# Rows of v with the head as the inner index: a P times V that reads every eighth value

## The chip, the cores and the metric

The kernel runs on one core of a Trainium2 chip. The metric is device time in microseconds (us) of one launch; lower is better. A profile of one execution on the chip stands beside the times.

## The reference

Attention with a local window and block summaries, and behind it a mixture of eight experts with two of them for each token. Only the attention matters here:

```python
B, H, S, D = q.shape                    # 4, 8, 768, 64
block, window = (32, 16)
k_sum = k.reshape(B, H, nb, block, D).max(axis=3)
v_sum = v.reshape(B, H, nb, block, D).mean(axis=3)
scores_l = scale * q @ k^T              # kept where |i - j| < window, else -1e9
scores_s = scale * q @ k_sum^T + log(block)
a = softmax(concat([scores_l, scores_s]))
out = a @ concat([v, v_sum])            # then the experts, on rows of (batch, token)
```

## The kernel before

The 4 x 768 tokens are worked through in 24 tiles of 128 tokens, each of two blocks of 64. A block sees a window of W = 94 keys and the NB = 24 block summaries, so NK = 118 keys. For one block and one head, P times V is a matmul with 118 keys on the partitions, the 64 tokens of P as the stationary operand and 65 columns of v as the moving one: the 64 values of the head and a column of ones, whose product is the sum of the softmax. With 8 heads and 2 blocks that is 16 matmuls for a tile, each of which the chip runs as two records because the type is fp32: 32 in the trace. They stand in `av` at line 329 (`L329`).

v comes from memory as rows of 8 heads x 65 values, 2080 bytes, with the ones already in them. They are used in two ways. `load_vn` (L138) brings a whole batch, six rows to a partition, for `v_sums` (L241), which sums blocks of 32 rows on PE. Its result, copied out of PSUM by DVE or ACT (L249, L247), gives the 24 rows of summaries at the top of six tiles `VW` a batch; further copies spread it over the six, on ACT and POOL for the first batch (L251, L253) and by transfers on chip (`v_rest`, L258) for the others. `v_window` (L263) brings 96 rows of v for one block under those 24 rows. The tiles are called `vw` in the trace, and those that lie in a buffer of the later stage `htl` (that of `load_vn` is `hth`).

The order of work is written out by hand. A loop over the tiles issues, in its turn `t`, the loads of v for tile `t + 2`, the scores of `t + 2`, the transposes of P for `t + 1`, the transposes of x for `t - 1` and P times V for `t`, with gate work of the experts in between at set places. All plain transfers are issued by SP in that order, and each waits for the one eight before it. Other lines that are named below: scores L296, mask L286, transposes of P L316 and their copy to SBUF L319 on ACT, transposes of x L366, gate logits L384, maximum of the scores L303 and normalisation L338 to L344 on DVE, the store of x L361.

Of the kernel before, what the change touches and what calls it, by code (L numbers as in the profile page):

```python
# [8 lines left out]
F32 = mybir.dt.float32  # L9
# [8 lines left out]
B, H, S, D = 4, 8, 768, 64  # L18
BLK, WIN = 32, 16
NB = S // BLK  # L20
P = 128
TS = S // P
NT = B * TS
N = B * S
DM = H * D
# [5 lines left out]
NK = W + NB  # L31
PAD = WIN - 1
KW = S + 2 * PAD + 2
VR = 96
VP = S + VR - 64
# [25 lines left out]
def attn_moe(ctx, tc, qt, kt, vt, wgn, noise, w1, w2, out):  # L61
    nc = tc.nc
# [15 lines left out]
    keep = attn.enter_context(tc.tile_pool(name="keep", bufs=1))  # L78
# [20 lines left out]
    KB, VW, KX = [], [], []  # L99
# [30 lines left out]
        kx_sum(t)  # L130

    flat = [x.rearrange("p f n -> p (f n)").bitcast(F32) for x in HT]
    VN = [flat[0][:, H * (D + 1) * j:H * (D + 1) * (j + 1)] for j in range(TS)]

    def load_vn(b, i):
        rows = vt[b, PAD:PAD + S].rearrange("(p j) h d -> p (j h d)", j=TS)
        c = slice(3 * H * (D + 1) * i, 3 * H * (D + 1) * (i + 1))
        nc.sync.dma_start(flat[0][:, c], rows[:, c])  # L138

    load_q(0)  # L140
# [60 lines left out]
        nc.gpsimd.memset(x[:, :, 0:PAD], 0.0)  # L201
        nc.gpsimd.memset(x[:, :, PAD + S:], 0.0)
    for i in range(2):
        VW += [keep.tile([P, H, D + 1], F32, name=f"vw{4 * i + j}") for j in range(4)]
        VW += [flat[1][:, H * (D + 1) * j:H * (D + 1) * (j + 1)].rearrange("p (h d) -> p h d", h=H)
               for j in range(2 * i, 2 * i + 2)]
    late = []
    XG = []
    for i in range(4):
        x = moe.tile([P, 2 * DM], F16, name=f"xg{i}")  # L210
# [21 lines left out]
            nc.tensor.matmul(o[:, i % 2, 0:P], identb, identb, start=True, stop=True, skip_group_check=True)  # L232
        VO.append(o)

    C4 = 2 * (D + 1)

    def v_sums(b):
        pt = psum.tile([P, HP, P], F32, name="pt", bufs=2).rearrange("p a b -> p (a b)")
        for j in range(TS):
            for g in range(4):  # L240
                nc.tensor.matmul(pt[32 * g:32 * g + NB, 0:C4], ind[:, j, :], VN[j][:, C4 * g:C4 * g + C4],  # L241
                                 start=(j == 0), stop=(j == TS - 1), skip_group_check=True)
        x = [y[0:NB].rearrange("p h d -> p (h d)") for y in VW[(b % 2) * 6:(b % 2) * 6 + 6]]
        for g in range(4):
            i, o = pt[32 * g:32 * g + NB, 0:C4], slice(C4 * g, C4 * g + C4)
            if b:
                nc.scalar.activation(x[0][:, o], i, AF.Copy)  # L247
            else:
                nc.vector.tensor_copy(x[0][:, o], i)  # L249
        if b == 0:  # L250
            nc.scalar.activation(x[1], x[0], AF.Copy)  # L251
            for i in range(2, 6):
                nc.gpsimd.tensor_copy(x[i], x[i % 2])  # L253

    def v_rest(b):
        x = [y[0:NB] for y in VW[(b % 2) * 6:(b % 2) * 6 + 6]]
        for y in x[1:]:
            nc.sync.dma_start(y, x[0])  # L258

    def v_window(blk):  # L260
        b, j = divmod(blk, 2 * TS)
        x = VW[(b % 2) * 6 + j % 6]
        nc.sync.dma_start(x[NB:NB + VR], vt[b, 64 * j:64 * j + VR])  # L263
        return x

    VX = {}

    def v_load(t):
        VX[t] = [v_window(2 * t), v_window(2 * t + 1)]

    SC, PE_, PT, PO, X, XR, XT = {}, {}, {}, {}, {}, {}, {}
# [52 lines left out]
    def av(t):  # L324
        o = PO[t]
        for h in range(H):
            for blk in range(2):
                c = (D + 1) * (h % 4)
                nc.tensor.matmul(o[64 * blk:64 * blk + 64, h // 4, c:c + D + 1],  # L329
                                 PT[t][:NK, h % 2, h // 2, 64 * blk:64 * blk + 64], VX[t][blk][:NK, h, :],  # L330
                                 start=True, stop=True, skip_group_check=True)

    xd_w = []
# [678 lines left out]
    for i in range(2):  # L1012
        load_vn(0, i)
# [9 lines left out]
    kx_sum(0)  # L1023
    q_piece(1)
    at(-0.9, v_sums, 0)

    w_alloc(0)
# [11 lines left out]
    for b in range(B - 1):  # L1039
        for j in range(TS):  # L1040
            at((6 * b + KP[j] if b else KP0[j]) + 0.1, k_piece, b + 1, j)
            if j % 3 == 0:
                at(6 * b + KL[j] if b else -1 + j // 3, load_k, b + 1, j, 3)
        for i in range(2):
            at(VL[b][i], load_vn, b + 1, i)
        at(VS[b] + 0.6, v_sums, b + 1)
        at(VS[b] + 1.02, v_rest, b + 1)
# [46 lines left out]
    for t in range(-2, NT - 1):  # L1094
# [45 lines left out]
        if t >= 0:  # L1140
            av(t)
# [5 lines left out]

    av_space(NT - 1)
    av(NT - 1)
    norm(NT - 2)  # L1150
    norm(NT - 1)
# [7 lines left out]
    for i in range(3):  # L1159
        x = late[0].tile([P, DM], F32, name=f"prev{i}")  # L1160
# [132 lines left out]
    for e in range(1, E):  # L1293
# [10 lines left out]
        d = 7 if e == 1 else 0  # L1304
# [117 lines left out]
def layout(q, k, v, moe_w_gate, moe_w_noise, moe_noise, moe_w1, moe_w2):  # L1422
    import numpy as np

    c = np.ascontiguousarray

    def heads(x):
        return c(x.reshape(B, HP, 2, S, D).transpose(0, 2, 4, 1, 3).reshape(B, 2 * D, HP, S))

    v1 = np.concatenate([v, np.ones((B, H, S, 1), v.dtype)], axis=3)  # L1430
    vp = np.zeros((B, VP, H, D + 1), v.dtype)
    vp[:, PAD:PAD + S] = v1.transpose(0, 2, 1, 3)
    wgn = np.zeros((P, DC, 4 * E), moe_w_gate.dtype)
    wgn[:, :, :2 * E] = np.concatenate([moe_w_gate, moe_w_noise], axis=1).reshape(DC, P, 2 * E).transpose(1, 0, 2)
    return {
        "qt": c(heads(q).reshape(B, 2 * D, HP, TS, P).transpose(0, 3, 1, 2, 4).reshape(B, TS, 2 * D, HP * P)),
        "kt": heads(k), "vt": vp,
        "wgn": c(wgn),
        "noise": c(moe_noise.reshape(NT, P, E).transpose(1, 0, 2)), "w1": c(moe_w1), "w2": c(moe_w2),
    }  # L1440
# [16 lines left out]
```

## Time and profile before

| | |
|---|---|
| median of 3 runs | 676.38 us (675.77 to 677.49) |
| the profiled execution | 674.24 us |
| its span, first to last instruction | 672.4 us |
| mean granted TensorE clock | 0.989 |
| PE, DVE, ACT, POOL busy | 640.2, 491.4, 318.9, 322.7 us |

The attention stage ends near 140 us, when the last P times V has run; what follows is the experts' work. The span does not hold the start and the end of the launch, which is the difference to the profiled execution's time. Busy time is the union of an engine's instructions. An idle time is put down to what ended it.

### The profile page before, as it was taken

To read this page: it belongs to the slowest core of one execution; us is meant where nothing else is said; L and a number is where in the kernel's file an instruction comes from. 1 tells how busy PE (TensorE), PEld (TensorE's weight loads), DVE (VectorE), ACT (ScalarE), POOL (GpSimd) and SP (SyncE) were. 2 spreads that over 40 slices of the span, in tenths; PEclk is the share of its full clock that TensorE was granted. 3 is DMA by queue.
4 is the path that set the end of the run, shared out by engine and by line. 5 is a ranking of instruction groups with operands and counts; after the bars stand their busy time and mean duration, and the time that the engine had idled before them with its cause. 6 is when DMAs were issued, how large, how long until landed. Compare 5 with 4: busy or idle time off the path is not lost.

```text
span 672.4 us, 14084 instructions
## 1 busy us (share of the span) xinstructions
PE 640.2 (95%) x5408; PEld 370.4 (55%) x5408; DVE 491.4 (73%) x905; ACT 318.9 (47%) x679; POOL 322.7 (48%) x459
## 2 busy tenths in 40 slices
PE   7989888979999999999999999999999999999993
PEld 6767667755454654555455446544554555455442
DVE  5648898989789588687958795788678687946410
ACT  2878888844152464156326523542463156326100
POOL 3354334430746646563856376545647551640141
PEclk9999999989999999999999999999999999999997
DMA  8999999869998866627554574567266622431121
GB/s 290 308 282 311 290 314 282 258 141 325 285 213 174 262 166 163 235 97 200 157 174 169 158 205 152 179 158 236 96 175 162 221 83 91 171 110 32 34 80 36
DMA packets 99242, 125.66 MB, mean 187 GB/s; under 512 B 57929, under 2 KB 62801, under 8 KB 99164
## 3 DMA queue, kind: packets, MB, share of 16 engines
q1 hardware_dynamic: 87020, 88.37, 45.0%
q0 software_dynamic: 12144, 36.28, 17.4%
q8 instruction: 45, 0.74, 0.5%
q14 instruction: 33, 0.27, 0.1%
HBM read 87.57 MB, written 26.21 MB: 169 GB/s over the span
## 4 chain that ended last, share of the span: by engine, by line
PE 80%; DVE 7%; DMA 6%; ACT 5%; issue 1%; SPq 0%; POOL 0%; POOLq 0%; DVEq 0%
PE pt L946 36%; PE h L827 26%; PE a L827 4%; PE h L791 4%; PE pt L943 3%; ACT p L310 2%; DMA stg<-in_w_dram 1%; PE pt L316 1%; DMA xg<-xd,tb 1%; DMA vw<-in_vt_dram 1%; DVE rh L541 1%; PE s L296 1%; DVE nm L303 1%; PE pt L241 1%; ACT pts L319 1%
## 5 line engine op out<-in xcount | busy, mean ns | idle before, releaser
L92 POOL DMA_INDIRECT out_dram<-y,tb x48 | 64.9, 1352 | 156.0 <-DVE y L969 147.9
L946 PEld LDWEIGHTS <-hth 128*128 128x128 f16 x768 | 75.0, 98 | 89.1
L92 POOL DMA_INDIRECT xg<-xd,tb x53 | 70.2, 1325 | 45.4 <-DVE oc L567 26.7
L946 PE MATMUL pt<-w2l,hth 128*128 128x512 f16 x376 | 88.8, 379 | 0.0
L946 PE MATMUL pt<-w2h,hth 128*128 128x512 f16 x376 | 88.8, 379 | 0.0
L946 PE MATMUL pt<-w2h,htl 128*128 128x512 f16 x376 | 88.8, 379 | 0.0
L827 PE MATMUL h<-tx,sh 128*128 128x408 f16 x336 | 78.7, 336 | 0.0
L969 DVE SCALAR_TENSOR_TENSOR y<-pt,tb,prev 128x512 f32<-128x512 f32 x42 | 31.5, 749 | 52.0 <-PE pt L946 52.0
L649 DVE SCALAR_TENSOR_TENSOR w2l<-stg,w2h 128x1024 f16<-128x1024 f32 x32 | 48.6, 1528 | 27.9 <-ACT w2h L632 27.9
L946 PEld LDWEIGHTS <-htl 128*128 128x128 f16 x384 | 37.6, 98 | 45.3
L827 PEld LDWEIGHTS <-w1h 128*128 128x128 f16 x448 | 43.2, 98 | 33.8 <-issue 1.4
L696 POOL TENSOR_TENSOR t<-xte 128x816 f32<-128x816 f16 x24 | 41.2, 1741 | 36.8 <-DVE t L652 32.3
L92 POOL DMA_INDIRECT prev<-out_dram,tb x42 | 51.9, 1236 | 12.7 <-issue 12.7
L827 PE MATMUL h<-xte,w1h 128*128 128x408 f16 x224 | 57.0, 336 | 0.0
L358 POOL TENSOR_TENSOR xr<-x,xr 128x512 f16<-128x512 f32 x22 | 25.6, 1163 | 61.0 <-ACT xr L351 27.0
L310 ACT ACTIVATE p<-s,nm 128x118 f32<-128x118 f32 x192 | 53.4, 377 | 0.8
L849 ACT ACTIVATE p<-h 128x408 f32<-128x408 f32 x28 | 14.3, 510 | 73.9 <-PE h L827 72.4
L724 ACT ACTIVATE tx<-t 128x816 f16<-128x816 f32 x28 | 24.0, 879 | 50.8 <-DVE t L652 50.8
L827 PEld LDWEIGHTS <-sh 128*128 128x128 f16 x336 | 32.9, 98 | 25.2 <-issue 0.2
L827 PE MATMUL h<-tx,sl 128*128 128x408 f16 x168 | 42.7, 336 | 0.0
L835 DVE SCALAR_TENSOR_TENSOR htl<-h,hth 128x408 f16<-128x408 f32 x56 | 32.1, 573 | 8.4 <-ACT hth L832 8.4
L677 ACT ACTIVATE sh<-ws 128x1536 f16<-128x1536 f32 x14 | 20.8, 1483 | 35.8 <-DVE ws L652 31.7
(213 smaller groups left out, 1239.9 us busy)
## 6 DMA issues: line engine op xcount, KB each, us to landing
stg<-in_w_dram SPq DMA_DIRECT2D x62, 512.0 KB
hth<-in_vt_dram SPq DMA_DIRECT2D x8, 780.0 KB
vw<-in_vt_dram SPq DMA_DIRECT2D x32, 195.0 KB
q<-in_qt_dram SPq DMA_DIRECT2D x24, 256.0 KB
xd<-xr SPq DMA_DIRECT2D x24, 256.0 KB
out_dram<-prev SPq DMA_DIRECT2D x8, 768.0 KB
kb<-in_kt_dram SPq DMA_DIRECT2D x6, 768.0 KB
htl<-in_vt_dram SPq DMA_DIRECT2D x16, 195.0 KB
```

Of the source, the lines that this page charges most:

```text
L92: return nc.gpsimd.indirect_dma_start(**kw)
L310: nc.scalar.activation(PE_[t][:, a, hp, :], SC[t][:, a, hp, :], AF.Exp, bias=NM[t][:, 1, a, hp:hp + 1], scale=0.125)
L358: engine.tensor_tensor(XR[t][:, DM:], X[t], XR[t][:, 0:DM], op=OP.subtract)
L649: nc.vector.scalar_tensor_tensor(lo, SG[e, i], sc, hi, op0=OP.mult, op1=OP.subtract)
L677: nc.scalar.activation(h, x, AF.Copy, scale=W1S)
L696: nc.gpsimd.tensor_tensor(tt(e, 0 if low else j), xb(e, *i, low), xb(e, *o, low), op=OP.subtract)
L724: nc.scalar.activation(TX[e][:, 0, j - 1], t_of(e, j), AF.Copy)
L791: nc.tensor.matmul(ph[:, :n], w[wn][:, c, f * P:(f + 1) * P], x[:, xo + c, c0:c1], start=(k == 0), stop=(k == 11), skip_group_check=hook i ...
L827: nc.tensor.matmul(o, lhs[a][:, c], rhs[b][:, c], start=start and n == 0, stop=stop and n == 5, skip_group_check=True)
L835: nc.vector.scalar_tensor_tensor(HT[1][:, f, c0:c1], c, 0.0, HT[0][:, f, c0:c1], op0=OP.max, op1=OP.subtract)
L946: nc.tensor.matmul(py, hx[:, f, c * P:c * P + P], w[:, f, :], start=first, stop=final, skip_group_check=True)
L969: nc.vector.scalar_tensor_tensor(y, py[:, :d], gw, pv[:, :d], op0=OP.mult, op1=OP.add)
```

## The change

Rows of v in memory now have the head as the inner index: 64 values of the head dimension, each for 8 heads, 2048 bytes a row. The column of ones is no longer loaded. It stands in the tiles `VW` as the last 8 values of each partition, written once at the start by POOL: 1 in all rows and then 32 in the 24 rows of summaries. P times V of one head takes its 65 columns as every eighth value of the row. Loads and copies of v move 512 values instead of 520, and `v_sums` works on 128 columns instead of 130.

```diff
-    VN = [flat[0][:, H * (D + 1) * j:H * (D + 1) * (j + 1)] for j in range(TS)]
+    VN = [flat[0][:, DM * j:DM * (j + 1)] for j in range(TS)]
     def load_vn(b, i):
-        rows = vt[b, PAD:PAD + S].rearrange("(p j) h d -> p (j h d)", j=TS)
-        c = slice(3 * H * (D + 1) * i, 3 * H * (D + 1) * (i + 1))
+        rows = vt[b, PAD:PAD + S].rearrange("(p j) d -> p (j d)", j=TS)
+        c = slice(3 * DM * i, 3 * DM * (i + 1))
...
-        VW += [keep.tile([P, H, D + 1], F32, name=f"vw{4 * i + j}") for j in range(4)]
-        VW += [flat[1][:, H * (D + 1) * j:H * (D + 1) * (j + 1)].rearrange("p (h d) -> p h d", h=H)
+        VW += [keep.tile([P, D + 1, H], F32, name=f"vw{4 * i + j}") for j in range(4)]
+        VW += [flat[1][:, H * (D + 1) * j:H * (D + 1) * (j + 1)].rearrange("p (d h) -> p d h", h=H)
                for j in range(2 * i, 2 * i + 2)]
+    for x in VW:
+        nc.gpsimd.memset(x[:, D, :], 1.0)
+        nc.gpsimd.memset(x[0:NB, D, :], float(BLK))
...
-    C4 = 2 * (D + 1)
+    C4 = DM // 4
...
-        x = [y[0:NB].rearrange("p h d -> p (h d)") for y in VW[(b % 2) * 6:(b % 2) * 6 + 6]]
+        x = [y[0:NB].rearrange("p d h -> p (d h)")[:, 0:DM] for y in VW[(b % 2) * 6:(b % 2) * 6 + 6]]
...
-        nc.sync.dma_start(x[NB:NB + VR], vt[b, 64 * j:64 * j + VR])
+        nc.sync.dma_start(x[NB:NB + VR].rearrange("p d h -> p (d h)")[:, 0:DM], vt[b, 64 * j:64 * j + VR])
...
-                                 PT[t][:NK, h % 2, h // 2, 64 * blk:64 * blk + 64], VX[t][blk][:NK, h, :],
+                                 PT[t][:NK, h % 2, h // 2, 64 * blk:64 * blk + 64], VX[t][blk][:NK, :, h],
...
-    vp = np.zeros((B, VP, H, D + 1), v.dtype)
-    vp[:, PAD:PAD + S] = v1.transpose(0, 2, 1, 3)
+    vp = np.zeros((B, VP, D * H), v.dtype)
+    vp[:, PAD:PAD + S] = v.transpose(0, 2, 3, 1).reshape(B, S, D * H)
```

The order of the instructions on POOL at the start of the program, before the change, from the last memset of the k buffers on (`xg` is a buffer of the later gather, `kx` the keys of a tile):

```order
L202 MEMSET kb_93 128x4x17
L212 MEMSET xg_163 128x1024
L579 IOTA steps 128x21
L119 COPY kx_96<-kb_92 128x4x94 [waits DMAHW2_49,DMAHW1_49]
L119 COPY kx_96<-kb_92 128x4x94
L253 COPY vw_154<-vw_152 24x520 [waits DVE_49]
```

The same place after the change, the last three of the twelve pairs of memsets and what follows (the first pair stands right behind the memset of `kb_93`):

```order
L208 MEMSET vw_159 128x8
L209 MEMSET vw_159 24x8 [waits Pool_49]
L208 MEMSET htl 128x8
L209 MEMSET htl 24x8 [waits Pool_49]
L208 MEMSET htl 128x8
L209 MEMSET htl 24x8 [waits Pool_49]
L215 MEMSET xg_187 128x1024
L582 IOTA steps 128x21
L119 COPY kx_96<-kb_92 128x4x94 [waits DMAHW2_49,DMAHW1_49]
```

Twenty-four instructions came in between; the copy for the third tile's keys still waits for the loads of k alone.

On PE, in the first P times V and behind it, before the change (the two `vw` are the tile's two blocks):

```order
L329 MATMUL o<-vw_152,pts 64x65 [waits DMAHW0_49]
L329 MATMUL o<-vw_153,pts 64x65 [waits DMAHW1_49]
L329 MATMUL o<-vw_152,pts 64x65
L329 MATMUL o<-vw_153,pts 64x65
L329 MATMUL o<-vw_152,pts 64x65
```

And after it:

```order
L332 MATMUL o<-vw_152,pts 64x65 [waits DMAHW0_49]
L332 MATMUL o<-vw_153,pts 64x65 [waits DMAHW1_49]
L332 MATMUL o<-vw_152,pts 64x65
L332 MATMUL o<-vw_153,pts 64x65
L332 MATMUL o<-vw_152,pts 64x65
```

Nothing moved here: the same matmuls wait for the same transfers, and the row does not show the step between the values. On SP the transfers keep their places too; the window loads are 96x512 instead of 96x520.

## Rows read from the trace of the kernel before

**Rows 1.** The page's first lines: span, and busy time, share of the span and number of instructions of each engine.
```profile
span 672.4 us, 14084 instructions
PE 640.2 (95%) x5408; PEld 370.4 (55%) x5408; DVE 491.4 (73%) x905; ACT 318.9 (47%) x679; POOL 322.7 (48%) x459
```

**Rows 2.** Busy time of each engine in the attention stage and behind it: the stretch, its length, then busy us (and instructions) of PE, PE's weight loads, DVE, ACT and POOL, the granted clock, the DMA share and GB/s.
```profile
20.00:140.00 120.00, 107.88 (x2148) 84.26 (x2142) 98.16 (x282) 103.58 (x323) 57.43 (x89) 1.00 0.93 286
140.00:672.40 532.40, 516.64 (x3030) 272.62 (x3024) 382.61 (x591) 209.51 (x339) 259.88 (x346) 0.99 0.55 161
```

**Rows 3.** PE's instructions in order of time for one turn of the loop over tiles: start, time from the first to the end of the last, line, operation, tiles, shape and count, and in brackets the idle time before it and what ended it.
```profile
62.33 1.15 PE L329 MATMUL o<-htl,pts 118*64 118x65 f32 x32
63.42 1.04 PE L296 MATMUL s<-kx,q 64*64 64x118 f32 x32
64.39 1.27 PE L316 MATMUL pt<-ident,p 128*118 128x128 f32 x8
65.59 0.35 PE L286 MATMUL s<-mask,identb 64*64 64x376 bf16 x4
66.34 1.08 PE L384 MATMUL pt<-xt,wg 128*32 128x128 f32 x32 [0.40 <-ACT pts L319]
67.35 0.66 PE L366 MATMUL pt<-ident,x 128*128 128x128 f32 x4
```

**Rows 4.** Who waited for whom from 20 to 140 us: the waiting engine, tile and line, what ended the wait, us in total, times, the longest.
```profile
POOL xr L358 <- ACT xr L351: 27.0, 10, 4.2
...
DVE r L338 <- PE o L329: 9.0, 6, 3.6
...
PE pt L366 <- ACT pts L319: 3.6, 9, 0.9
...
POOL xr L358 <- DMA vw<-vw: 3.3, 1, 3.3
POOL xr L358 <- DMA xd<-xr: 2.8, 1, 2.8
...
PE pt L384 <- ACT pts L319: 2.3, 4, 0.9
...
PE pt L384 <- issue: 1.1, 1, 1.1
PE pt L241 <- ACT pts L319: 1.0, 2, 0.8
...
PE pt L241 <- issue: 0.9, 1, 0.9
...
DVE xr L355 <- DMA xd<-xr: 0.6, 1, 0.6
```

**Rows 5.** The records of P times V: durations in ns (least, median, most), and the first and last start in us.
```profile
L329 PE MATMUL o<-vw,pts x480: 219/222/271, 22.4 to 136.0; 118*64 118x65 f32 x160
L329 PE MATMUL s<-htl,pts x32: 219/222/223, 139.6 to 140.5; 118*64 118x65 f32 x32
```

**Rows 6.** The same of the gate's matmuls.
```profile
L384 PE MATMUL pt<-xt,wg x192: 272/273/298, 45.8 to 144.3; 128*32 128x128 f32 x192
```

**Rows 7.** The transfers of v in the whole program: target and source, queue, count, KB each.
```profile
hth<-in_vt_dram SPq DMA_DIRECT2D x8, 780.0 KB
vw<-in_vt_dram SPq DMA_DIRECT2D x32, 195.0 KB
htl<-in_vt_dram SPq DMA_DIRECT2D x16, 195.0 KB
```

**Rows 8.** All transfers from 12 to 133 us.
```profile
DMA packets 17729, 35.47 MB, mean 293 GB/s; under 512 B 1939, under 2 KB 5267, under 8 KB 17704
```

**Rows 9.** Transfers from 14 to 17 us, when window loads of v make up nearly all of it.
```profile
DMA packets 434, 0.78 MB, mean 261 GB/s; under 512 B 61, under 2 KB 61, under 8 KB 434
```

**Rows 10.** Transfers from 115 to 117 us, when rows of 2048 bytes of q and of the experts' weights make up nearly all of it.
```profile
DMA packets 412, 0.78 MB, mean 389 GB/s; under 512 B 32, under 2 KB 32, under 8 KB 412
```

**Rows 11.** POOL's instructions at the start of the program, columns as in rows 3.
```profile
2.24 0.29 POOL L184 TENSOR_SCALAR base<-base 128x8 f32<-128x8 f32 x1
2.60 0.21 POOL L186 COPY bs<-base 128x8 f32<-128x8 f32 x1
...
4.34 0.15 POOL L202 MEMSET kb<- 128x68 f32 x1
4.43 0.94 POOL L212 MEMSET xg<- 128x1024 f16 x1
5.33 0.15 POOL L579 IOTA steps<- 128x21 f32 x1
7.76 0.94 POOL L119 COPY kx<-kb 128x376 f32<-128x376 f32 x2 [2.28 <-DMA kb<-in_kt_dram]
20.24 1.28 POOL L253 COPY vw<-vw 24x520 f32<-24x520 f32 x2 [11.54 <-DVE vw L249]
```

**Rows 12.** PE's sums of v for one batch, columns as in rows 3.
```profile
71.54 1.53 PE L241 MATMUL pt<-hth 128*24 128x130 f32 x48 [0.18 <-ACT pts L319]
```

**Rows 13.** The chain of work that ended last, followed back from the end, in order of time around 52 to 75 us: start, length, engine or transfer and line.
```profile
52.54 8.98 DMA stg<-in_w_dram
...
61.59 7.27 DMA vw<-in_vt_dram
...
68.92 5.97 DMA xd<-xr
```

More of the change, by code (lines that the diff above doesn't have):

```diff
@@ L255, in v_rest @@
     def v_rest(b):
-        x = [y[0:NB] for y in VW[(b % 2) * 6:(b % 2) * 6 + 6]]
+        x = [y[0:NB].rearrange("p d h -> p (d h)")[:, 0:DM] for y in VW[(b % 2) * 6:(b % 2) * 6 + 6]]
         for y in x[1:]:
@@ L1428, in heads @@
         return c(x.reshape(B, HP, 2, S, D).transpose(0, 2, 4, 1, 3).reshape(B, 2 * D, HP, S))
-    v1 = np.concatenate([v, np.ones((B, H, S, 1), v.dtype)], axis=3)
-    vp = np.zeros((B, VP, H, D + 1), v.dtype)
-    vp[:, PAD:PAD + S] = v1.transpose(0, 2, 1, 3)
+    vp = np.zeros((B, VP, D * H), v.dtype)
+    vp[:, PAD:PAD + S] = v.transpose(0, 2, 3, 1).reshape(B, S, D * H)
     wgn = np.zeros((P, DC, 4 * E), moe_w_gate.dtype)
```

## The prediction

> **What bounds the kernel now.** I read the page's first lines, then the two halves of the span, then one tile's turn on PE, then who waits for whom. The span is 672.4 us, with PE busy for 95% of it [rows 1]. The change touches only what works with v, so the stretch that counts is the attention stage. [...] Three engines and the transfers are nearly level there; PE is the fullest and has 12.1 us free. From 140 us on nothing reads v.
>
> One turn of PE [rows 3] shows the order: P times V (L329, 1.15 us), the next scores (L296), transposes of P (L316), mask (L286), sometimes gate work (L384), transposes of x (L366), and the next P times V. It runs back to back; the gap is a wait for the copy of the transposed P on ACT. Those waits are 3.6 + 2.3 + 1.0 = 6.9 us between 20 and 140 us, and two more gaps of 1.1 and 0.9 us are put down to issue [rows 4]. Whatever makes L329 longer makes the turn longer, except where it eats such a wait. Engines hardly wait for transfers: DVE waits 0.6 us for a store, and POOL 3.3 and 2.8 us, on a step that waits 27.0 us for ACT alone [rows 4].
>
> **The read of every eighth value.** The matmuls of a tile are the same, 32 records in the same order, and only the moving operand changes: 65 values that lay side by side now lie 32 bytes apart. The 32 take 1.15 us [rows 3]; one alone takes 0.222 us [rows 5], which is the tail of the last, so 1.15 - 0.22 = 0.93 us is the time in which values stream in. That is 32 x 65 / 0.93 = 2.2 values per ns.
>
> No PE instruction of before reads with such a step, so the price is bounded. Below: the step costs nothing, 0. A gain is excluded, since the number of columns is the same. Above: the memory must pass over all bytes between the values. The most that a row shows PE reading is L384, 32 matmuls of 128 columns in 1.08 us, of which 0.27 us is the tail [rows 3, 6]: 32 x 128 x 4 bytes / 0.81 us = 20 bytes per ns and partition. P times V would have to pass over 2.2 x 32 = 72 bytes per ns at its old pace, so it would be 3.6 times slower: 0.93 becomes 3.3 us, +2.4 us a tile. Between ends of 1 and 3.6 I take the geometric middle, 1.9, rounded to 2: +0.93 us a tile, since L384 shows that contiguous reads have about twice the room (5.1 values per ns against 2.2) and that no row shows room for 72. Over 24 tiles: 24 x 0.93 = 22 us more of PE.
>
> [...]
>
> What of the 22 us reaches the end: ACT is not the fullest engine, and a longer P times V gives it time to finish the copies for which PE now waits. I let 6 of the 6.9 us of such waits [rows 4] go, so the stage grows by 22 - 6 = 16 us. Behind the longer L329 stand the scores of the next tile (L296), on which DVE's maximum and then ACT's exponentials wait; DVE's normalisation waits for L329 itself already, 9.0 us in 6 waits [rows 4]. Those are parts of the same turn and add nothing of their own.
>
> **The shorter rows.** 48 window loads of 96 rows and 8 loads of 128 runs [rows 7] lose 32 bytes a row (96 a run): 4608 x 32 + 1024 x 96 = 246 KB out of 35.47 MB in 12 to 133 us [rows 8], 0.7%, or 0.8 us of the queue at its 293 GB/s. That is the least. At most, v's rows reach the pace of rows of 2048 bytes: with nearly only v rows in flight the engines move 261 GB/s [rows 9], with nearly only 2048-byte rows 389 GB/s [rows 10]. 48 x 195 KB is 9.58 MB, 37 us at the one and 24 us at the other rate (9.44 MB), so 13 us less. Either way it frees DMA engines, and what waits for them is the little named above. Cover: v for a tile is asked for two tiles ahead. I count 0 in the likeliest case, where PE is slower still and transfers have more time.
>
> **The small edits.** POOL gets 24 memsets after L202. Small memsets there start 0.09 us apart [rows 11], which gives 24 x 0.09 = 2.2 us as the least; every second one waits on the one before, and a dependent pair of steps on POOL is 0.36 us apart in the same rows (L184 to L186), which gives 12 x (0.09 + 0.36) = 5.4 us as the most. The next POOL work begins at 7.76 us, when k lands, and then POOL idles 11.54 us [rows 11]. At the most the copy at 7.76 starts near 10.9 us, for a third tile whose scores are not due before 20 us. Cost 0; without that idle time it would be up to 3.1 us. The window loads wait on no memset. The sums (L241) have 128 columns instead of 130: 1.5% of 1.53 us in each of four batches [rows 12], under 0.1 us together. The copies on DVE, ACT and POOL shrink from 520 to 512 values: nothing.
>
> **Sum.** The profiled execution took 674.2 us for its span of 672.4; the median of the runs is 676.4, 2.1 us above it. 674.2 + 16 = 690 on the profiled one, 676.4 + 16 = 692.4 as a median. I call 692.
>
> **Rivals.**
> - *Nothing moves*: PE reads every eighth value at the old pace and the lighter queue was hidden anyway. For it: the rate of an fp32 stream here is already low, and L384 shows room for twice the contiguous values. Against: each value now stands 32 bytes from the next. 676 us, within 0.5 us.
> - *Faster*: the old pace holds, and the lighter queue takes away what it holds up: DVE's wait of 0.6 us [rows 4] and PE's issue gaps of 1.1 + 0.9 us [rows 4], if those are late instructions that come over the same DMA engines. The chain of work runs through three transfers from 52.5 to 74.9 us [rows 13], which speaks for it; that hardly an engine idles there speaks against. 676.4 - 2.6 = 673.8 us. It decides if P times V stays under 1.2 us a tile. [...]
> - *A small penalty*: factor 1.3, +0.28 x 24 = 6.7 us, most of it in waits that vanish: 678 to 680 us.
> - *The upper bound*: +2.4 us a tile, 57 us, less 7 us of waits: about 726 us.
> - *The change does not do what it says for transfers*: the v loads have 96 partitions where the fast ones have 128, so their lower rate may come from that and not from 2080 bytes. Then the DMA gain is 0.8 us; this removes the faster case and moves no other.
>
> **How the numbers follow.** Likeliest, factor near 2: 0.48, with its own range 686 to 701 (all 12 us of free time absorbed: 676.4 + 22 - 12 = 686; none absorbed and a factor a little over 2: 676.4 + 24 = 701). Small penalty 0.09. Nothing moves 0.22. Faster 0.15. Upper bound 0.06. The range 674 to 701 leaves out the upper bound, most of the faster case and the edges of the others, about 2 in 10. About 2 us, 0.3%, is what a measurement of this kernel can tell from no change. Faster 0.15, same 0.22, slower 0.48 + 0.09 + 0.06 = 0.63.
>
> **What would show it.** In the trace after, the 32 matmuls of P times V take about 2.1 us a tile instead of 1.15, with one alone near 0.28 us; 1.15 again proves that step wrong and leaves the first two rivals. PE's busy time from 20 us to the end of the stage grows by about 22 us, its waits on ACT's copies shrink, and the last P times V ends 16 us later than its 140.5 + 0.2 us of before [rows 5]. The DMA share of the stage falls. What comes after is shifted and not changed. The forecast fails if the penalty is absent or if the free time of PE takes more of it than 12 us.

## The result, and the profile after

The median went from 676.93 us (675.77 to 678.29) to 683.69 us (683.10 to 684.24): ratio 1.0099, 95% interval 1.0076 to 1.0122. The change costs 6.8 us. The forecast was slower by 15.6 us, so the sign is right and the size is not. The profiled execution of after took 683.36 us. Its line numbers are 3 higher than those of before from L241 on: P times V is L332, the scores L299, the transposes of P L319 and their copy L322, the transposes of x L369, the gate L387.

The page's first lines of after, which answer to [rows 1]:

```profile
span 681.6 us, 14108 instructions
PE 656.5 (96%) x5408; PEld 387.4 (57%) x5408; DVE 490.0 (72%) x905; ACT 320.3 (47%) x679; POOL 323.2 (47%) x483
```

PE's busy time grew by 16.3 us, DVE's and ACT's by nothing. The two stretches of after, columns as in [rows 2]:

```profile
20.00:140.00 120.00, 117.66 (x2015) 95.47 (x2019) 90.29 (x262) 98.44 (x304) 52.21 (x83) 1.00 0.90 277
140.00:681.60 541.60, 523.68 (x3145) 279.18 (x3135) 387.89 (x610) 215.11 (x357) 263.26 (x350) 0.99 0.55 160
```

PE is idle for 2.3 of 120 us, where it was idle for 12.1. The two stretches are equally long, so that of after holds less of the work (2015 records of PE against 2148). The DMA share fell from 0.93 to 0.90, as the same work is spread over more time. A turn of PE in after, columns as in [rows 3]:

```profile
59.40 2.12 PE L332 MATMUL o<-vw,pts 118*64 118x65 f32 x32
61.45 1.04 PE L299 MATMUL s<-kx,q 64*64 64x118 f32 x32
62.41 1.09 PE L319 MATMUL pt<-ident,p 128*118 128x128 f32 x8
...
64.42 2.12 PE L332 MATMUL o<-htl,pts 118*64 118x65 f32 x32
```

P times V takes 2.12 us instead of 1.15, and the scores take what they took; the transposes of P take 1.09 us, where they took 1.27. No gap is left in this turn, which has no gate work. The records of P times V, which answer to [rows 5]:

```profile
L332 PE MATMUL o<-vw,pts x480: 298/299/313, 21.3 to 144.9; 118*64 118x65 f32 x160
...
L332 PE MATMUL s<-htl,pts x32: 298/299/303, 149.1 to 150.9; 118*64 118x65 f32 x32
```

The last P times V ends at 150.9 + 0.3 = 151.2 us instead of 140.7: the stage ends 10.5 us later. Who waited for whom from 20 to 145 us in after, columns as in [rows 4]:

```profile
DVE r L341 <- PE o L332: 18.8, 12, 3.7
ACT pts L322 <- PE pt L319: 11.9, 14, 2.2
...
PE pt L387 <- ACT pts L322: 0.7, 2, 0.5
...
PE pt L369 <- ACT pts L322: 0.5, 3, 0.2
```

The waits have turned round. PE waited 3.6 + 2.3 us for ACT's copies before [rows 4] and waits 0.5 + 0.7 us now; DVE's normalisation waits 18.8 us for P times V where it waited 9.0, and ACT's copies, which waited 2.4 us for PE before, now wait 11.9.

One difference between the profiled executions is not the change's. The profiled execution of before lies 2.7 us below the median of before in this comparison (674.24 and 676.93), that of after 0.3 us below its own. So the traces differ by 9.1 us and the medians by 6.8. Where a size is judged below, the medians decide.

### The profile page after: what moved, and what is told of

It reads as the page before. It is cut to its first block, busy times and chain, and to the rows that moved or that the text cites. A ratio compares the mean times of both kernels' runs of the same rounds, so it can differ in the third digit from the quotient of the medians.

```text
span 681.6 us, 14108 instructions
## 1 busy us (share of the span) xinstructions
PE 656.5 (96%) x5408; PEld 387.4 (57%) x5408; DVE 490.0 (72%) x905; ACT 320.3 (47%) x679; POOL 323.2 (47%) x483
## 4 chain that ended last, share of the span: by engine, by line
PE 89%; DVE 5%; ACT 2%; DMA 1%; issue 1%; SPq 0%; POOL 0%; POOLq 0%; DVEq 0%
PE pt L949 36%; PE h L830 26%; PE o L332 5%; PE a L830 4%; PE h L794 3%; PE pt L946 3%; PE pt L319 3%; PE s L299 3%; PE pt L369 2%; DMA kb<-in_kt_dram 1%; PE pt L244 1%; PE h L949 1%; PE pt L387 1%; ACT p L313 1%; DVE nm L306 1%; ACT pts L322 1%
```

## The experiments

Times are medians, ratios are against runs of before on the same chip, which took 675.89 us beside e1 to e3, 675.02 beside e4 to e7, 677.84 beside e8 to e11 and 677.65 beside e12 and e13. The letters of the theories belong to each expectation; the text names the theories in words.

### e1: the long rows kept, the strided read too

After, with the ones loaded again: rows of 2080 bytes, the head as the inner index, no memsets.

```diff
-    vp = np.zeros((B, VP, D * H), v.dtype)
-    vp[:, PAD:PAD + S] = v.transpose(0, 2, 3, 1).reshape(B, S, D * H)
+    vp = np.zeros((B, VP, (D + 1) * H), v.dtype)
+    vp[:, PAD:PAD + S] = v1.transpose(0, 2, 3, 1).reshape(B, S, (D + 1) * H)
```

> The changed kernel with one part undone: P times V still reads every eighth value, but the rows of v in memory are 2080 bytes again, with the ones in their last 8 values, and the memsets are gone. Theory 1 (the strided read costs 23 us of PE, free time of PE swallows 13 of them, and the length of the rows is worth nothing): 683 to 685 us, as the changed kernel. Rival (the free time swallows only the 6 us that were forecast, and the shorter rows give about 8 us back): 690 to 693 us.

Measured: 681.58 us, ratio 1.0095 (1.0062 to 1.0129), where after has 1.0099. The loss comes with the read; beside it the shorter rows and the memsets show no effect, though the two ratios are compared to no better than about 3 us.

### e2, e10 and e11: the short rows alone

e2 has the rows of 2048 bytes and the ones written on chip, but the heads lie one behind the other and P times V reads 65 values side by side. The 65th column is then another head's value for all heads but the last, so all heads are divided by the sum of head 7. e10 is before with that same division and nothing else; e11 is e2 again, beside e10.

```diff
-  PT[t][:NK, h % 2, h // 2, 64 * blk:64 * blk + 64], VX[t][blk][:NK, h, :],
+  PT[t][:NK, h % 2, h // 2, 64 * blk:64 * blk + 64], VX[t][blk].rearrange("p d h -> p (d h)")[:NK, D * h:D * h + D + 1],
...
-        nc.vector.tensor_scalar(r, o[:, :, :, D], 1e-9, 1.0 / XS, op0=OP.add, op1=OP.mult)
+        nc.vector.tensor_scalar(r, o[:, 1:2, 3:4, D].to_broadcast([P, 2, 4]), 1e-9, 1.0 / XS, op0=OP.add, op1=OP.mult)
```

> The other part alone: rows of 2048 bytes, ones on chip, but with the 64 values of a head side by side, so that P times V reads 65 neighbours as before. The column of ones stands behind the last head only, so all heads are divided by the sum of head 7; the amount of work is the same. Theory 1 (row length is worth nothing where PE sets the pace): 676 to 678 us, like the kernel before. Rival (shorter rows give 6 to 8 us back): 668 to 671 us.

> The kernel before, with all heads divided by the sum of head 7, as in e2, so the output is not that of the reference; nothing else. If e2's 0.3% came from its 2048-byte rows, this takes the time of before within 0.5 us. If it came from the other read of the sums, this is 1.5 to 2.5 us faster than before, as e2 was.

> The same kernel as e2 on the chip of e10 (heads divided by the sum of head 7): 2048-byte rows, ones on chip, contiguous read. If the rows are worth something, 0.2 to 0.4% faster than before and than e10 again; if not, equal to e10.

Measured: e2 673.19 us, ratio 0.9967 (0.9945 to 0.9990). e10 677.00, ratio 0.9991 (0.9961 to 1.0021). e11 674.70, ratio 0.9960 (0.9930 to 0.9990). From e10 to e11 the means of 12 runs each differ by 2.3 us, with an interval of 0.4 to 4.2. So the gain of about 0.3% belongs to the rows with what goes with them (the ones written on chip, 512 values instead of 520), and not to the division. Part of the 2.3 us may be the granted clock: its mean over the runs is 0.9891 in e10 and 0.9902 in e11, and within one kernel the runs with a lower mean are mostly the longer ones (correlation -0.61 in e10 and -0.74 in e11). A straight line through the runs of this chip (about 0.6 us for 0.001, an estimate) leaves 1.6 us, 0.2 to 3.1, for the rows. Beside the strided read no such gain shows, but e1 is not exact enough to exclude it there. Where in the trace it arises is not settled: from 20 to 140 us PE is busy 105.5 us in e10 and 105.4 in e11, and ACT 102.9 and 102.3. From 140 to 160 us the granted clock is 0.91 in e10 and 1.00 in e11, but it is 1.00 in e4 too, which has the long rows.

### e0: what a step costs on PE

Matmuls on constants and nothing else of the kernel. Each group reads its moving operand with a step of 1, 2, 3, 4, 8 or 16 elements, in the shape of P times V (65 fp32 columns on the two 64-column halves of the array in turn), on one half alone, on four quarters, and with fp16 on the whole array.

```python
mf[s] = pool.tile([P, 128, s], F32, name="f" + words[s])
...
nc.tensor.matmul(o[64 * b:64 * b + 64, 0, 0:65], wf[:118, 0:64], mf[s][:118, 0:65, i % s], start=True,
                 stop=True, skip_group_check=True)
```

> Nothing of the program is left but matmuls on constant tiles, to price the read by itself: fp32 in two column strips as in P times V, in one strip and in four, and fp16 over the full array, each with steps of 1, 2, 3, 4, 8 and 16 values. [...] If it hangs on the bytes passed over: steps 2, 3 and 4 already cost, and 16 costs more than 8. If it is a limit of the memory shared by the strips: one strip with step 8 is free, and four strips cost twice what two do.

PE's instructions in order of time, columns as in [rows 3]; the name of the moving tile says the step. First fp32 on both halves, then on one half, then fp16 on the whole array:

```profile
10.30 2.09 PE L86 MATMUL o<-fone,wf 118*64 118x65 f32 x64
12.21 2.09 PE L86 MATMUL o<-ftwo,wf 118*64 118x65 f32 x64
14.13 3.04 PE L86 MATMUL o<-fthree,wf 118*64 118x65 f32 x64
17.00 4.01 PE L86 MATMUL o<-ffour,wf 118*64 118x65 f32 x64
20.83 4.02 PE L86 MATMUL o<-feight,wf 118*64 118x65 f32 x64
24.67 4.13 PE L86 MATMUL o<-fsixteen,wf 118*64 118x65 f32 x64
28.61 2.05 PE L90 MATMUL o<-fone,wf 118*64 118x65 f32 x32
30.49 2.04 PE L90 MATMUL o<-ftwo,wf 118*64 118x65 f32 x32
...
38.93 4.02 PE L90 MATMUL o<-feight,wf 118*64 118x65 f32 x32
42.77 3.79 PE L90 MATMUL o<-fsixteen,wf 118*64 118x65 f32 x32
...
63.98 3.67 PE L99 MATMUL o<-hone,wh 128*128 128x256 f16 x32
67.48 3.79 PE L99 MATMUL o<-htwo,wh 128*128 128x256 f16 x32
71.11 5.59 PE L99 MATMUL o<-hthree,wh 128*128 128x256 f16 x32
76.54 7.42 PE L99 MATMUL o<-hfour,wh 128*128 128x256 f16 x32
83.78 14.63 PE L99 MATMUL o<-height,wh 128*128 128x256 f16 x32
98.23 14.90 PE L99 MATMUL o<-hsixteen,wh 128*128 128x256 f16 x32
```

A group of 32 matmuls on both halves has 64 records in fp32, one of 32 in fp16 has 32. Read the differences of the starts. In fp32 step 2 costs what step 1 costs (1.92 and 1.91 us), step 3 half as much again (2.87), step 4 twice (3.83), and steps 8 and 16 hardly more than step 4 (3.84 us; 4.13 from first to end against 4.01). So from step 4 on the price does not grow with the bytes passed over, which was the prediction's way to its upper bound. At step 8 one half alone needs as long for its 32 records (3.84 us) as both halves for their 64, and at step 1 nearly so (1.88 us against 1.91). One half takes 32 x 65 values in a group: 0.92 ns a value at step 1, 1.84 ns from step 4 on. In fp16 a group is 32 x 256 values: 0.43 ns each at step 1, then 0.44, 0.66, 0.88 and 1.76 ns at steps 2, 3, 4 and 8. Past the steps that cost nothing, the time of a value grows with the step: in fp32 it is 1.38 and 1.84 ns at 12 and 16 bytes, 0.115 ns a byte, and in fp16 0.66, 0.88 and 1.76 ns at 6, 8 and 16 bytes, 0.11 ns a byte (both an estimate from these rows). Beyond 16 bytes it hardly grows in either (in fp16 14.90 us from first to end at step 16 against 14.63 at step 8). Of the expectation, neither a price by the bytes passed over nor a limit shared by the strips came out: step 2 costs nothing and step 16 hardly more than step 8, and one half at step 8 is not free (3.84 us against 1.88 at step 1).

### e4 and e5: the dose of the strided read

e4 interleaves the heads in pairs, so that P times V reads every second value. e5 interleaves heads 0 to 3 by four and leaves 4 to 7 as before, which is half of after's extra work on PE. Both have rows of 2080 bytes with the ones.

```diff
+    lo = v1[:, :4].transpose(0, 2, 3, 1).reshape(B, S, 4 * (D + 1))
+    hi = v1[:, 4:].transpose(0, 2, 1, 3).reshape(B, S, 4 * (D + 1))
+    vp[:, PAD:PAD + S] = np.concatenate([lo, hi], axis=2)
```

> As the run with strided reads and rows of 2080 bytes, but the heads are interleaved in pairs, so that P times V reads every second value (8 bytes apart). By the table of steps this read is free: one tile's P times V takes 1.15 us and the time is that of the kernel before, 675 to 678 us. If any step costs: 679 us or more.

> Rows of 2080 bytes; heads 0 to 3 are interleaved by four (16 bytes apart, the full price by the table of steps), heads 4 to 7 lie side by side. PE has 24 x 0.48 = 11.5 us more to do than before. Theory A (PE's free time of about 13 us in the stage is used up first, and only what is left over arrives): 676 to 678 us. Theory B (a fixed share of about a third arrives, whatever the size): 679 to 681 us.

Measured: e4 674.43 us, ratio 0.9999 (0.9981 to 1.0017), so step 2 is free in the kernel as in e0. e5 676.19, ratio 1.0024 (1.0006 to 1.0042): of 11.5 us of extra work on PE 1.2 arrive (0.4 to 2.8). That is the 676 to 678 us of free time that is used up first, and below the 679 of a fixed share.

### e3: every P times V twice

Before, with each matmul of P times V issued twice: PE's work of after without its read.

```diff
-        for h in range(H):
+        for h in 2 * list(range(H)):
```

> The kernel before with every matmul of P times V issued twice in a row, 64 records a tile instead of 32, with neighbouring values: as much more PE time as the strided read costs (0.93 to 1.0 us a tile, 23 us in all) without a stride and without any change to the transfers. Theory 1 (the free time of PE in the stage swallows 13 of any 23 us): 683 to 686 us. Rival (it swallows 6, and something else in the change gave the rest back): 690 to 693 us.

Measured: 693.09 us, ratio 1.0258 (1.0222 to 1.0294), where e1, beside it, took 681.58. That is above the 683 to 686 expected, and about the 690 to 693 named beside them, but by another cause than the one named there. It is not a clean dose. From 84 us on its turns (from one P times V to the next) are those of e1 within 0.1 us, but for one of 6.45 us against 5.96; the loss stands in the early tiles. Its busy times in three stretches, then PE's waits from 15 to 85 us:

```profile
20.00:60.00 40.00, 33.68 (x780) 27.79 (x784) 18.98 (x37) 26.59 (x83) 16.08 (x27) 1.00 0.92 270
60.00:80.00 20.00, 16.45 (x311) 13.38 (x305) 12.33 (x37) 13.45 (x43) 8.33 (x12) 0.83 0.78 255
80.00:145.00 65.00, 63.72 (x1467) 53.06 (x1467) 54.41 (x161) 51.42 (x157) 24.16 (x35) 1.00 0.81 245
```

```profile
PE pt L316 <- issue: 3.4, 1, 3.4
...
PE pt L241 <- DMA hth<-in_vt_dram: 2.0, 1, 2.0
...
PE pt L241 <- issue: 1.8, 1, 1.8
```

PE is idle for 6.3 and 3.6 us in the first two stretches and for 1.3 in the third; the granted clock falls to 0.83 in the second, beside such idle time. That the 768 added records come late as instructions was not shown. More work on PE is better added with the same number of instructions, and the next runs do so.

### e6 and e7: a larger dose in other lines

The transposes of P (L316) and of x (L366, all but those of the last two tiles) read an identity whose values stand 16 bytes apart, in before (e6) and in after (e7). The number of instructions stays.

```diff
+    wide = flat[1][:, 2304:2816].rearrange("p (a b) -> p a b", b=4)[:, :, 0]
+    nc.vector.tensor_scalar(wide, ji, 0.0, None, op0=OP.is_equal)
...
-            nc.tensor.transpose(pt[:NK, hp, :], PE_[t][:, a, hp, :], ident)
+            nc.tensor.transpose(pt[:NK, hp, :], PE_[t][:, a, hp, :], wide)
```

> The kernel before, whose transposes of P and x read an identity spread out in steps of 16 bytes: the same number of instructions and transfers, and 12 x 0.107 = 1.28 us more for PE in a tile, 31 us in all, if the price of the step is a second slot for each of 128 columns. Theory A: 31 - 13 = 18 us more, 693 to 696 us. Theory B: 10 us more, 685 to 688 us.

> The same spread identity in the changed kernel: 23 + 31 = 54 us more for PE than before. Theory A: the free time is gone already, so nearly all of the 31 us arrives on top of the changed kernel's 683: 710 to 716 us. Theory B: a third of 54, 18 us over the kernel before: 693 to 696 us.

Measured: e6 686.35 us, ratio 1.0178 (1.0155 to 1.0201); e7 707.64, ratio 1.0496 (1.0474 to 1.0518). e6 came out at the 685 to 688 of a fixed share, e7 near the 710 to 716 of a pool: neither theory holds over all doses. The dose was a little larger than the 31 us named: 0.94 us a tile in the transposes of P (0.117 us for each of the eight, where the expectation put 0.107) and 0.45 in those of x, 32.5 us in all.

| | extra PE work, us | time against before, us | taken up, us | extra work in a turn, us | usual short turn, us |
|---|---|---|---|---|---|
| before | 0 | 0 | 0 | 0 | 4.06 |
| e5 | 11.5 | 1.2 | 10.3 | 0.48 | 4.45 |
| after | 23.3 | 6.8 | 16.5 | 0.97 | 4.95 |
| e6 | 32.5 | 11.3 | 21.2 | 1.39 | 5.33 |
| e7 | 55.8 | 32.6 | 23.2 | 2.36 | 6.30 |

A turn is the time from one P times V to the next. Two short ones, of e6 and of e7 (5.34 and 6.31 us), columns as in [rows 3]:

```profile
28.97 1.15 PE L331 MATMUL o<-vw,pts 118*64 118x65 f32 x32
...
34.31 1.15 PE L331 MATMUL o<-htl,pts 118*64 118x65 f32 x32
```

```profile
27.77 2.12 PE L334 MATMUL o<-vw,pts 118*64 118x65 f32 x32
...
34.08 2.12 PE L334 MATMUL o<-htl,pts 118*64 118x65 f32 x32
```

In the short turns the differences agree: 4.45 - 0.48, 4.95 - 0.97, 5.33 - 1.39 and 6.30 - 2.36 are all 3.94 to 3.98 us. That is PE's own work in such a turn; where own work and dose together pass the turn's old length, the turn becomes longer by the rest. In before the nine shortest turns took 4.06 to 4.87 us; together they went from 40.0 to 45.1 us in after. The nine longest (5.6 to 7.1 us, most with gate work or the sums of v) went from 56.7 to 57.7 us together, though one of them from 6.29 to 7.98. The other turns, with the end of the stage, took 4.5 us more, 2.4 of them in one turn in which PE waits 1.5 us for DVE in this execution and not in e1. Single turns must be read with care: that of 6.29 us takes 7.66 in e4 and 7.55 in e10, whose P times V costs what it costs in before.

### e8, e9, e12 and e13: the same dose in short and in long turns

The spread identity only in nine turns, the nine shortest or the nine longest of before. In e8 and e9 the transposes of P alone, in e12 and e13 those of x too.

```diff
-            nc.tensor.transpose(pt[:NK, hp, :], PE_[t][:, a, hp, :], ident)
+            nc.tensor.transpose(pt[:NK, hp, :], PE_[t][:, a, hp, :], wide if t - 2 in (0,1,2,5,6,7,10,14,18) else ident)
...
-            nc.tensor.transpose(pt[:, c], X[t][:, c * P:(c + 1) * P], ident)
+            nc.tensor.transpose(pt[:, c], X[t][:, c * P:(c + 1) * P], wide if t in (0,1,2,5,6,7,10,14,18) else ident)
```

> The kernel before; in nine turns of the loop the eight transposes of P read an identity whose values stand 16 bytes apart. The nine are those that were shortest before (4.06 to 4.87 us from one P times V to the next). Dose: 9 x 0.94 = 8.5 us of PE (L318 took 2.03 us a tile so in e6, 1.09 before). Theory A, each turn has its own slack and pays what exceeds it: PE's own work fills about 3.95 us of such a turn (5.33 in e6 less its 1.39 us of dose), so the turns go to 4.9 us, a sum of about 4 us, of which the next long turns give some back: +2.5 to +4 us. Theory B, one pool of about 10 us over the stage: 0 to +1 us. Theory C, a fixed share of about 0.3: +2.5 us, as in e9.

> As e8, the same dose of 8.5 us, in the nine turns that were longest before (5.61 to 7.08 us). Theory A: 0 to +1.5 us, since PE's own work does not fill these turns (the price that shows in after's turns of the same tiles is 1.0 us in all, from the one with the sums of v). Theory B: 0 to +1 us. Theory C: +2.5 us.

Measured: e8 678.38 us, ratio 1.0013 (0.9983 to 1.0043); e9 677.44, ratio 0.9995 (0.9962 to 1.0028). They tell nothing apart: the two conditions counted from the wrong tile (t - 1 where t - 2 was meant), so each dose fell one turn too early, and both kernels had short and long turns among the nine. e12 and e13 put it right, with more work.

> The kernel before; the transposes of P and of x that lie in the nine shortest turns of before (4.06 to 4.87 us from one P times V to the next) read the identity whose values stand 16 bytes apart. Dose: 9 x 1.39 = 12.5 us of PE (1.39 us a turn in e6, which dosed all turns). Theory A, each turn has its own free time and pays what exceeds it: the nine turns go to 5.3 to 5.8 us as in e6, where they were longer than before by 8.6 us in all; of that the long turns behind give back up to 1 us: +7 to +9 us. Theory B, one pool of about 10 us: +2.5 us. Theory C, a fixed share (e6: 11.7 of 31): +4.7 us.

> The same dose of 12.5 us in the nine longest turns of before (5.61 to 7.08 us). Theory A: these nine were 2.6 us longer in e6 than before: +1 to +3 us. Theory B: +2.5 us. Theory C: +4.7 us. A holds if this is at least 4 us below e12; B and C want the two equal.

Measured: e12 680.28 us (676.08 to 684.80, 12 runs), ratio 1.0025 (0.9994 to 1.0056); e13 678.15, ratio 1.0010 (0.9982 to 1.0039). The means differ by 1.7 us, with an interval of 0 to 3.4. That misses the 7 to 9 us of turns that each pay for themselves, and the 4 us between the two kernels; the pool's 2.5 us holds for e12, and its interval leaves room for it in e13. The traces show why. PE in e12 from the first turns on, columns as in [rows 3], and the long turn of the same stretch in before:

```profile
23.26 1.16 PE L331 MATMUL o<-vw,pts 118*64 118x65 f32 x32
...
28.69 1.15 PE L331 MATMUL o<-vw,pts 118*64 118x65 f32 x32
...
34.02 1.15 PE L331 MATMUL o<-htl,pts 118*64 118x65 f32 x32
...
39.35 1.16 PE L331 MATMUL o<-vw,pts 118*64 118x65 f32 x32
...
42.75 1.53 PE L243 MATMUL pt<-hth 128*24 128x130 f32 x48
...
44.79 0.40 PE L331 MATMUL o<-vw,pts 118*64 118x65 f32 x6
```

```profile
34.90 1.15 PE L329 MATMUL o<-vw,pts 118*64 118x65 f32 x32
...
38.53 0.64 PE L241 MATMUL pt<-hth 128*24 128x130 f32 x14
40.07 1.27 PE L241 MATMUL pt<-hth 128*24 128x130 f32 x34 [0.90 <-issue]
...
41.86 1.15 PE L329 MATMUL o<-vw,pts 118*64 118x65 f32 x32
```

The three dosed turns take 5.43, 5.33 and 5.33 us, as the 3.95 us of own work say: together 16.09 us instead of 12.49 (22.41 to 34.90 us in before), so they pay 3.6 us. The next, long turn is not dosed and takes 5.44 us instead of 6.96: the gap of 0.90 us in the sums of v is gone, and so is other waiting. E12's nine dosed turns grow by 8.7 us together and the nine long ones shrink by 3.2 (one of them grows). What PE loses in a short turn it gets back in part in a long one, probably because what the long one waited for was on its way meanwhile. So the free time is shared between neighbouring turns.

Whether the place of a dose counts at all can't be told from the 1.7 us, since the granted clock differs too: its mean is 0.9895 over e12's runs and 0.9913 over e13's, and e12's runs go from 684.80 us at 0.986 to 676.08 at 0.994. With a straight line for the clock through these runs and those of before beside them (0.7 us for 0.001, an estimate), e12 costs 3.5 us and e13 3.1, which differ by 0.4 (-0.6 to 1.5). So no price of the place is shown: both doses of 12.5 us cost about 3 us. If a dose itself lowers the clock, this way of counting would hide it: in the trace of e12 PE waits 2.1 us for DVE at the end of the stage, and the granted clock from 140 to 160 us is 0.91.

## Why the prediction was wrong in size

**The read.** Right, with the value chosen: factor 2, +0.97 us a tile against +0.93, one record 299 ns against the 280 named, 23.3 us in all against 22. The reasoning towards it was only half right, so that the hit is in part luck: the value was the middle between two bounds, and the upper one (all bytes passed over, 3.6 times) does not hold, since e0 shows the price nearly flat from step 4 on (3.83, 3.84 and 3.94 us a group). With the heads interleaved by 4 instead of 8 a head costs the same (e5: half of the heads, 0.48 us a tile), and by 2 nothing (e4).

**What of it reaches the end.** This is the step that failed: "I let 6 of the 6.9 us of such waits [rows 4] go, so the stage grows by 22 - 6 = 16 us." By the medians 16.5 us were taken up: 23.3 us of more work gave 6.8 us of more time. The traces show two sources beyond the 6 us. From the start of the first P times V to the end of the last, columns as in [rows 2], in before:

```profile
22.40:140.70 118.30, 106.38 (x2142) 83.64 (x2138) 97.40 (x282) 101.39 (x317) 56.03 (x86) 1.00 0.93 285
```

And in after:

```profile
21.30:151.20 129.90, 125.72 (x2143) 102.82 (x2140) 95.34 (x282) 103.19 (x317) 56.88 (x90) 1.00 0.90 271
```

The stretch holds the same instructions and is 11.6 us longer. First, PE's idle time falls by 7.7 us, from 11.9 to 4.2: the wait rows on ACT's copies, 6.9 us, were taken for all that could vanish, while 12.1 us of idle time stood in [rows 2] beside them. Second, the idle time was itself not all: PE's busy time grew by 19.3 us where its work grew by 23.3, so about 4.0 us of what counted as busy before was waiting, a term that the prediction put at nothing. It shows in groups of matmuls whose first waits hide behind long records, as in the transposes of P: between 20 and 140 us 184 records keep PE busy for 28.07 us in before, and 172 for 23.91 us in after. For a tile's 8 records that is 1.22 us before and 1.11 after; [rows 3] had one of 1.27, and the turn of after has 1.09.

So these two traces show 7.7 + 4.0 = 11.7 us of free time used. Of the other 4.8 us, 1.1 lie ahead of the stretch, which starts earlier in after, 1.3 behind it, and 2.4 are the difference between these two executions and the medians; that the change made them is not shown. Executions differ by as much: the stretch of before takes 119.2 us in e4 and 121.9 in e10, whose P times V costs the same, and that of after takes 127.8 in e1. The likeliest case's own range began at 686, with "all 12 us of free time absorbed", and that limit was too low for the same reason; with e7 the part taken up reaches 23 us. The prediction's last sentence named this as what would break it.

**The shorter rows.** 0 was right for this kernel (e1), though not because rows are worth nothing: without the strided read they gain 2.3 us (e11 against e10), near the 2.6 us of the faster case, whose mechanism no trace shows. That PE as the bound covers the gain in after fits, but is only argued. The rival on the loads fits as well: rows of 2048 bytes alone do not bring the window loads near the 389 GB/s of [rows 10]. That their 96 partitions are the reason was not tested. All transfers of after from 14 to 17 us, the stretch of [rows 9]:

```profile
DMA packets 461, 0.81 MB, mean 271 GB/s; under 512 B 68, under 2 KB 79, under 8 KB 461
```

**The small edits.** Right. The 24 memsets stand in POOL's idle time; here the first, the last and the copy they were to delay, columns as in [rows 11]:

```profile
4.42 0.10 POOL L208 MEMSET vw<- 128x8 f32 x1
...
6.69 0.10 POOL L209 MEMSET htl<- 24x8 f32 x1
...
7.74 0.94 POOL L119 COPY kx<-kb 128x376 f32<-128x376 f32 x2
```

They take 4.42 to 6.79 us, 2.4 us, and the copy starts at 7.74 us where it started at 7.76.

**What comes behind.** Shifted and not changed, but for the handover: the first matmuls of the experts wait 1.44 us for their gathered tokens before and start 8.7 us later in after without a wait, so 1.8 of the 10.5 us by which the stage ends later go no further. This belongs to the execution of before more than to the change: its experts start 5.6 us after the last P times V, and those of after, e4 and e10 start 3.8 to 3.9 us after it. In before:

```profile
146.26 1.44 PE L791 MATMUL h<-xte,w1h 128*128 128x384 f16 x4 [1.44 <-DMA xte<-xg]
```

In after:

```profile
154.95 0.81 PE L794 MATMUL h<-xte,w1h 128*128 128x384 f16 x4
```

**The rivals.** "Nothing moves" and "faster" needed P times V under 1.2 us a tile and fell with its 2.12. "A small penalty" (678 to 680 us) came nearer to the time than the forecast, by a factor of 1.3 that was not there.

What stays open, beside the 4.8 us that the two traces leave: which engine or transfer bounds the long turns one by one, so that the taken-up part could have been worked out from before's rows alone; where the 2.3 us of the short rows arise; and why e3 loses its early tiles.

## What to carry to other kernels

In the shapes measured here (e0), the moving operand of an fp32 matmul streams as fast with a step of 8 bytes as side by side (0.92 ns a value), an fp16 one with a step of 4 bytes (0.44 ns against 0.43); with a step of 16 bytes a value takes 1.84 and 1.76 ns, 2 and 4 times as long, and a wider step costs hardly more. Lay the values out accordingly. Where several engines are nearly level, do not take the busiest one's idle time, let alone its named waits, for its free time: subtract its plain work, turn by turn (here 3.95 us of turns of 4.06 to 7.1 us), since waits inside a group count as busy. Extra work makes a turn longer only where the sum passes the turn's length, and neighbouring turns share what is free (e12). One trace does not give the free time to the us: the same stretch with equal work took 118.3, 119.2 and 121.9 us in three executions (before, e4, e10).

## What the runs showed of the hardware beyond that

In e0 the time of the fp16 matmuls of step 8 stayed the same while the granted clock fell. The clock was 0.71 on average in the first half of the group and 0.50 in the second, and all 32 records took 629 to 632 ns. Mean granted clock is the third number from the end:

```profile
83.80:91.00 7.20, 7.20 (x17) 1.93 (x16) 0.00 (x0) 0.00 (x0) 0.71 0.00 0
91.00:98.20 7.20, 7.20 (x17) 2.02 (x16) 0.00 (x0) 0.00 (x0) 0.50 0.00 0
```

```profile
L99 PE MATMUL o<-height,wh x32: 629/630/632, 83.8 to 97.8; 128*128 128x256 f16 x32
```

PE had run fp16 matmuls at wider and wider steps without a break when the clock fell; from 76.6 to 83.7 us, in step 4, it was still 1.00. In after's attention stage, with 2.12 us a tile for P times V among other work, it was 1.00 from 20 to 140 us.
